# The last two blocks of a windowed-attention kernel: P turned on TensorE instead of by a DMA, and another order of the closing chains

## The chip, the cores and the metric

The kernel runs on one core of a Trainium2 chip. The metric is the device time of one execution in microseconds; lower is better. Before the change three runs gave 814.06, 810.92 and 812.58 us, a median of 812.58 us.

## The reference

```python
xn = layernorm(x)                                   # x: 1 x 2048 x 640
q  = (xn @ wq) -> 32 heads of 192                    # wq: 640 x 6144
k, v = last 512 rows of k_cache, v_cache             # per head 512 x 192
p  = softmax(q @ k.T * 192**-0.5)                    # per head 2048 x 512
s  = concat(p @ v) @ wo                              # wo: 6144 x 640
r  = xn @ w_r;  idx = the two rows with the largest r
y  = (silu(xn[idx] @ w_gate) * (xn[idx] @ w_up)) @ w_down * sigmoid(r[idx])
g  = silu(xn + y added into rows idx)
out = x + s * g
```

Nearly all of the work is attention: 32 heads, 2048 tokens, a window of 512 keys, and the projections into and out of the heads. The two-row expert part is small and lies long before the end.

## The kernel before

Heads are taken in pairs. A *step* is a group of four heads, a span of 512 tokens and a pair of heads; it is cut into two *blocks* of 256 tokens (two token tiles, a = 0 and 1, of 128 tokens). There are 64 steps and 128 blocks. A block b does, for each of its two token tiles, the scores (S, line 366, six matmuls into a PSUM tile of two banks), their row maximum on VectorE (M, line 371), and the exponentials on ScalarE (E, line 376, two instructions, one for each head). The exponentials are written as bf16 into `p_ring`, a ring of two blocks. The product with V needs P with the keys on the partitions, so P has to be turned. Line 380 does that for both token tiles with one DMA transpose on SP's queue (sixteen 128 x 128 tiles), issued behind the second E of the block, into `pT_ring`, a ring of three blocks.

Two blocks later P V is multiplied (called P or O in the order, line 393, 32 matmuls into two PSUM banks). A column of ones in V gives the softmax's sum beside the product. VectorE takes its reciprocal (line 400), and the product is scaled, for one head by VectorE (line 404) and for the other by ScalarE (line 407), into `o_ring`. The scaled O is turned as well, by a DMA transpose of six tiles (line 410), or, for the last two blocks, on TensorE (T, line 420, six transposes) with a copy out of PSUM by ScalarE (line 421). Six blocks later the output projection (W, line 434, 24 matmuls) reads turned O of two blocks: items 120 and 121 read blocks 120 and 122, items 122 and 123 read blocks 121 and 123, items 124 and 125 read blocks 124 and 126, items 126 and 127 read blocks 125 and 127. An item is half of the 640 output columns for two token tiles u = 0 and 1.

In the last head group each item is finished at once: VectorE multiplies it with g (line 460, one instruction for each u), and GpSimd adds `s_acc`, which by then holds x plus all earlier groups (line 465, a full row of 640 columns, after the odd item). The result goes out by DMA on GpSimd's queue, for the last four token tiles on SP's (line 466). Items 126 and 127 add their halves by themselves (line 462), on GpSimd for 126 and on VectorE for 127, and send them on SP's and ScalarE's queues (line 463).

PSUM is four pools: two tiles of two banks for scores ("s"), one tile of two banks for the q projection ("q"), two single banks for O and W ("o"). A W item or a turned tile of the end may be put into any of them; it then waits for the reader of the tile that stood there.

The order of the instructions on every engine is the order in which the program issues them; nothing rearranges it. Blocks 12 to 125 follow `BLOCK`; blocks 126 and 127 and the closing work follow the tokens of `LAST`, read by `last()`. In a token such as `W.122.q` or `O.126.va` the first number is the block or item, letters behind it name the bank or the engines (v VectorE, a ScalarE). SP's queue works in order: a DMA that waits for its data holds back those behind it.

Of the kernel before, what the change touches and what calls it, by code (L numbers as in the profile page):

```python
# [9 lines left out]
ALU = mybir.AluOpType  # L10
AX = mybir.AxisListType
ET = mybir.EngineType
FP32 = mybir.dt.float32
BF16 = mybir.dt.bfloat16
# [7 lines left out]
def kernel(ctx, tc, A_x, A_k_cache, A_v_cache, A_wq, A_wo, B_x, B_w_r, B_w_gate, B_w_up, B_w_down, out):  # L22
    nc = tc.nc
    P = 128
    _, S, D = A_x.shape
# [3 lines left out]
    W = min(4096, max(256, Sk // 4))  # L29
# [11 lines left out]
    KB = W // HK  # L41
# [9 lines left out]
    out_v = out.flatten_outer_dims().rearrange("(n p) d -> p n d", p=P)  # L51
# [5 lines left out]
    def pool(name, bufs, **kw):  # L57
        return ctx.enter_context(tc.tile_pool(name=name, bufs=bufs, **kw))
# [10 lines left out]
    ps_s = pool("ps_s", 2, space=bass.MemoryType.PSUM)  # L69
# [4 lines left out]
    def f_tile(shape, dtype, name, kind="q"):  # L74
        return banks[kind].tile(shape, dtype, name=name, tag="f")
# [3 lines left out]
    s_acc = big.tile([P, NTB, D], FP32, name="s_acc")  # L79

    RP, RO, RT, RV, VC = 3, 3, 7, 3, Dh + 4
    p_ring = big.tile([P, 2, 2, KB, 2, HK], BF16, name="pexp")
    pT_ring = big.tile([P, RP, 2, KB, P], BF16, name="pT")
# [20 lines left out]
    def half(r):  # L104
        return slice(r * HK, (r + 1) * HK)
# [56 lines left out]
    for _ in range(22):  # L162
# [5 lines left out]
        out=ident_f, in_=ident_f, compare_op=ALU.not_equal, fill=1.0, base=0,  # L168
        pattern=[[-1, P]], channel_multiplier=1,
    )  # L170
    ident = const.tile([P, P], BF16, name="ident")
# [115 lines left out]
    NS = len(steps)  # L287
    NB = 2 * NS
    HEAD = 12
    qT_of = {}  # L290
    fin_x = {}
    fin_pool = {}
# [76 lines left out]
    def row_max(b, a):  # L369
        nm_of[b, a] = small.tile([P, 2], FP32, name="nm")  # L370
        rm = nc.vector.tensor_reduce(out=nm_of[b, a], in_=s_of[b, a], axis=AX.X, op=ALU.max, negate=True)  # L371
        last_max["ins"], last_max["S"] = rm.ins, s_no[b, a]

    def exps(b, a):
        for hh in range(2):
            nc.scalar.activation(out=p_ring[:, b % 2, a, :, hh, :].rearrange("p (x j) e -> p x j e", x=2),  # L376
                                 in_=s_of[b, a][:, hh, :].rearrange("p (j e x) -> p x j e", j=NJ, x=2),
                                 func=ACT.Exp, bias=nm_of[b, a][:, hh:hh + 1], scale=1.0)
        if a == 1:
            nc.sync.dma_start_transpose(out=pT_ring[:, b % RP].rearrange("p a k t -> p (a k) t"),  # L380
                                        in_=p_ring[:, b % 2].rearrange("p a k h e -> p (a k h e)"))

    o_of = {}

    def o_products(b, between=None):
        g, t5, pr = steps[b // 2]
        o_of[b] = [f_tile([P, 2, W // 2], FP32, "o_ps", "o") for _ in range(2)]
        for a in range(2):
            if a == 1 and between is not None:
                between()  # L390
            for k in range(KB):
                for r in range(2):
                    nc.tensor.matmul(o_of[b][r][:, a, 0:Dh + 1], lhsT=pT_ring[half(r), b % RP, a, k, :],  # L393
                                     rhs=v_ring[half(r), (g * PAIRS + pr) % RV, k, 0:Dh + 1],
                                     start=(k == 0), stop=(k == KB - 1))

    def o_scaled(b, engines):
        rl = small.tile([P, 2, 2], FP32, name="rl")
        for r, e in sorted(enumerate(engines), key=lambda c: c[1]):
            nc.vector.reciprocal(out=rl[:, r], in_=o_of[b][r][:, :, Dh])  # L400
            o_sb = o_ring[:, b % RO, 3 * r:3 * r + 3].rearrange("p c a e -> p a c e")
            src = o_of[b][r][:, :, 0:Dh].rearrange("p a (c e) -> p a c e", e=HK)
            if e == "v":
                nc.vector.tensor_tensor(out=o_sb, in0=src, in1=rl[:, r].unsqueeze(2).unsqueeze(3).to_broadcast([P, 2, 3, HK]), op=ALU.mult)  # L404
            else:
                for a in range(2):
                    nc.scalar.activation(out=o_sb[:, a], in_=src[:, a], func=ACT.Copy, scale=rl[:, r, a:a + 1])  # L407
# [16 lines left out]
    def w_of(k):  # L424
        sp, up, h = k // 4, (k // 2) % 2, k % 2
        g, t5 = divmod(sp, NT5)
        return g, t5 * 4 + 2 * up, slice(h * HD, (h + 1) * HD), [4 * sp + 2 * pr + up for pr in range(PAIRS)]

    def w_products(k, w_ps):
        g, n, cs, bs = w_of(k)  # L430
        for pr in range(PAIRS):
            for c in range(CC):
                for r in range(2):
                    nc.tensor.matmul(w_ps[r][:, 0:HD], lhsT=oT_ring[half(r), bs[pr] % RT, c, :], rhs=grp[g][("wo", pr)][half(r), c, cs],  # L434
                                     start=(pr == 0 and c == 0), stop=(pr == PAIRS - 1 and c == CC - 1))

    def fin_tiles(n):
        if n not in fin_t:
            fin_t[n] = (fin_pool["t"].tile([P, 2, D], FP32, name="fin_t"), [fin_pool["o"].tile([P, D], BF16, name="fin_o") for _ in range(2)])
        return fin_t[n]  # L440

    def w_item(k, act=False, where="o", last=False):
        g, n, cs, _ = w_of(k)
        if where == "o":
            w_ps = [f_tile([P, W], FP32, "w", "o") for _ in range(2)]
        else:
            w_t = f_tile([P, 2, W], FP32, "w") if where == "q" else ps_s.tile([P, 2, W], FP32, name="w", tag="sc")
            w_ps = [w_t[:, u] for u in range(2)]
        w_products(k, w_ps)
        for u in range(2):  # L450
            src, acc = w_ps[u][:, 0:HD], s_acc[:, n + u, cs]
            if g == 0 and act:
                nc.scalar.copy(out=acc, in_=src)
            elif g == 0:
                nc.vector.tensor_copy(out=acc, in_=src)
            elif g < NG - 1:
                nc.vector.tensor_tensor(out=acc, in0=acc, in1=src, op=ALU.add)  # L457
            else:
                t, o = fin_tiles(n)
                nc.vector.tensor_tensor(out=t[:, u, cs], in0=src, in1=xn[:, n + u, cs], op=ALU.mult)  # L460
                if last:
                    (nc.vector if k % 2 else nc.gpsimd).tensor_tensor(out=o[u][:, cs], in0=t[:, u, cs], in1=s_acc[:, n + u, cs], op=ALU.add)
                    (nc.sync, nc.scalar)[u].dma_start(out=out_v[:, n + u, cs], in_=o[u][:, cs])
                elif k % 2 == 1:
                    nc.gpsimd.tensor_tensor(out=o[u], in0=t[:, u], in1=s_acc[:, n + u, :], op=ALU.add)  # L465
                    (nc.sync if n >= NTB - 4 else nc.gpsimd).dma_start(out=out_v[:, n + u, :], in_=o[u])
# [41 lines left out]
    copies = {"a": nc.scalar.copy, "v": nc.vector.tensor_copy}  # L508
# [102 lines left out]
    M = {}  # L611
# [210 lines left out]
    def m_gate(n):  # L822
        def a():
            M["tz"] = M["s"].tile([P, D], FP32, name="tz", tag="t2")
            nc.scalar.activation(out=M["tz"], in_=xn[:, n, :], func=ACT.Tanh)

        def b():
            nc.vector.scalar_tensor_tensor(out=xn[:, n, :], in0=M["tz"], scalar=1.0, in1=xn[:, n, :], op0=ALU.add, op1=ALU.mult)
        return a, b
# [29 lines left out]
    for n in range(NTB):  # L859
        bg[71 + 2 * n].append(m_add(n))  # L860
        a, b = m_gate(n)
# [33 lines left out]
    banks["o"] = pool("ps_o", 2, space=bass.MemoryType.PSUM)  # L895
    for b in range(HEAD, NB - 2):
        for token in BLOCK:
# [11 lines left out]
            elif token == "P":  # L909
                def between():  # L910
                    for f in bg.pop(b, []):
                        f()
# [5 lines left out]
    def last(token):  # L918
        op, *n = token.split(".")
        e = n[-1] if n and n[-1].isalpha() else None  # L920
        n = [int(c) for c in n if not c.isalpha()]
        if op == "S":
            scores(*n)
        elif op == "M":
            row_max(*n)
        elif op == "E":
            exps(*n)
        elif op == "P":
            o_item(n[0], e)
        elif op == "O":  # L930
            o_products(n[0])
            o_scaled(n[0], e)
        elif op == "T":
            o_turn(n[0], copies[e])
        elif op == "W":
            w_item(n[0], where=e or "o", last=n[0] >= NB - 2)
        else:
            flush(n[0])

    LAST = """  # L940
    S.126.0 M.126.0 W.120 E.126.0 S.126.1 M.126.1 P.124.va E.126.1 B.126
    S.127.0 M.127.0 W.121.q E.127.0 P.125.va S.127.1 M.127.1 E.127.1 B.127
    W.122.q O.126.va W.123.s T.126.a O.127.va W.124.s T.127.a W.125.s W.126.q W.127
    """.split()
    for token in LAST:
        last(token)
# [31 lines left out]
```

## Time and profile before

| | |
|---|---|
| three runs | 810.92 to 814.06 us, median 812.58 us |
| profiled execution, own time | 812.12 us |
| its span | 810.3 us |
| TensorE clock granted, mean | 0.997 |
| TensorE busy | 784.5 us, 97% of the span |
| VectorE busy | 585.8 us, 72% |
| ScalarE busy | 528.2 us, 65% |
| GpSimd busy | 311.5 us, 38% |
| DMA queue with the transposes | 93.0% of 16 engines' span |

The profiled execution takes 1.8 us longer than its span, from the first to the last instruction. Times in what follows are us from the start of the span. A line of the timeline merges instructions of one kind that follow each other: start, duration, engine, line of the kernel, operation, tile written <- tiles read, count, and in square brackets the idle time of the engine before them and what ended it. In the lines by group the numbers behind the bar are busy us and the mean ns of one instruction, then idle time of the engine before them. "Landing" is the time from a DMA's issue to its completion.

### The profile page before, as it was taken

What the parts mean: (1) busy time and instruction counts of PE and PEld (TensorE: products, weight loads), DVE (VectorE), ACT (ScalarE), POOL (GpSimd) and SP (SyncE); (2) the same over time, 40 slices, a digit from 0 to 9 for tenths busy, and PEclk for the clock granted to TensorE, in tenths of its full rate; (3) what the DMA queues carried; (4) which work ended last, traced back from release to release, by engine and by line L of the source; (5) the groups of instructions that cost most, each with busy time, mean ns of one, the idle gap of its engine ahead of it and who ended that gap; (6) DMA issues with size and microseconds to landing.
All of it is one profiled execution on the core that took longest, in us unless ns stands there. A gap on an engine that the chain in (4) does not pass through costs nothing.

```text
span 810.3 us, 26575 instructions
## 1 busy us (share of the span) xinstructions
PE 784.5 (97%) x11338; PEld 580.1 (72%) x11338; DVE 585.8 (72%) x1083; ACT 528.2 (65%) x963; POOL 311.5 (38%) x244
## 2 busy tenths in 40 slices
PE   8799899999999999999999999999999999999995
PEld 4366577777777777777777777777777777777773
DVE  7686588887777767767767677777777776776673
ACT  5677566666656766666666667767777776666661
POOL 1312120011110101001011799959995423555854
PEclk9999999999999999999999999999999999999998
DMA  7997998799999999999998999989999899998983
GB/s 192 190 173 165 196 172 165 143 183 170 182 188 181 172 214 199 193 178 206 196 205 154 175 182 181 161 157 181 154 193 176 150 185 176 198 187 160 191 155 76
DMA packets 446807, 142.81 MB, mean 176 GB/s; under 512 B 414180, under 2 KB 446184, under 8 KB 446688
## 3 DMA queue, kind: packets, MB, share of 16 engines
q1 hardware_dynamic: 436912, 131.71, 93.0%
q10 hardware_dynamic: 8816, 6.88, 3.2%
q0 software_dynamic: 960, 2.52, 1.1%
q8 instruction: 89, 1.46, 0.7%
q14 instruction: 30, 0.25, 0.1%
HBM read 39.98 MB, written 2.62 MB: 53 GB/s over the span
## 4 chain that ended last, share of the span: by engine, by line
PE 84%; DMA 7%; DVE 4%; ACT 3%; issue 2%; POOL 0%; SPq 0%; DVEq 0%; ACTq 0%; POOLq 0%
PE w L434 23%; PE q_ps L339 21%; PE o_ps L393 18%; PE s L366 18%; DMA pT<-pexp 6%; DVE nm L371 2%; PE q_ps L308 2%; ACT pexp L376 1%; PE warm_ps L163 1%; DMA xnT<-xn 1%; ACT o_sb L407 1%; DMA wo_g<-in_A_wo_dram 1%; ACT qT L351 0%; ACT qT L314 0%; PE gu_ps L754 0%
## 5 line engine op out<-in xcount | busy, mean ns | idle before, releaser
L371 DVE TENSOR_REDUCE nm<-s 128x2 f32<-128x1024 f32 x256 | 313.0, 1223 | 138.0 <-PE s L366 130.9
L376 ACT ACTIVATE pexp<-s,nm 128x512 bf16<-128x512 f32 x512 | 323.6, 688 | 97.7 <-DVE nm L371 54.2
L339 PE MATMUL q_ps<-xnT,wq_g 64*128 64x512 bf16 (+1 forms) x2340 | 232.6, 323 | 3.7 <-ACT qT L351 1.5
L434 PE MATMUL w<-wo_g,oT 64*128 64x320 bf16 x3072 | 232.4, 297 | 2.4 <-ACT o_sb L407 2.1
L366 PE MATMUL s<-kT,qT 64*128 64x512 bf16 x1536 | 211.8, 376 | 5.1 <-ACT pexp L376 3.9
L434 PEld LDWEIGHTS <-oT 64*128 64x128 bf16 x3072 | 173.2, 94 | 60.5 <-issue 5.0
L393 PEld LDWEIGHTS <-pT 64*128 64x128 bf16 x4096 | 179.2, 94 | 33.7 <-DMA pT<-pexp 6.2
L393 PE MATMUL o_ps<-v_sb,pT 64*128 64x193 bf16 x4096 | 197.9, 243 | 4.6 <-DMA pT<-pexp 4.4
L407 ACT ACTIVATE o_sb<-o_ps,rl 128x192 bf16<-128x192 f32 x256 | 93.6, 417 | 142.5 <-DVE rl L400 139.7
L339 PEld LDWEIGHTS <-wq_g 64*128 64x128 bf16 x2340 | 127.8, 99 | 48.8 <-issue 3.2
L151 POOL COPY wo_g<-wo_g 64x1920 bf16<-64x1920 bf16 x32 | 59.4, 1861 | 221.8 <-DMA wo_g<-in_A_wo_dram 201.1
L366 PEld LDWEIGHTS <-qT 64*128 64x128 bf16 x1536 | 85.7, 94 | 59.4 <-issue 6.0
L457 DVE TENSOR_TENSOR s_acc<-s_acc,w 128x320 f32<-128x320 f32 x192 | 85.0, 484 | 34.2 <-PE w L434 34.2
L351 ACT ACTIVATE qT<-q_ps 128x1024 bf16<-128x1024 f32 x114 | 92.4, 810 | 6.6 <-PE q_ps L339 1.9
L121 POOL COPY k_perm<-k_raw 128x768 bf16<-128x768 bf16 x30 | 25.0, 851 | 143.3 <-DMA k_raw<-in_A_k_cache_dram 110.8
L404 DVE TENSOR_TENSOR o_sb<-o_ps,rl 128x384 bf16<-128x384 f32 x128 | 71.4, 557 | 4.6 <-DVE rl L400 0.2
L818 POOL TENSOR_SCALAR yh<-y_bc,oh 128x640 bf16<-128x640 bf16 x32 | 60.8, 1901 | 3.3 <-DMA y_bc<-y_d 1.7
L819 POOL TENSOR_TENSOR xn<-xn,yh 128x640 bf16<-128x640 bf16 x32 | 45.4, 1418 | 2.7
L400 DVE RECIPROCAL rl<-o_ps 128x2 f32<-128x2 f32 x256 | 30.0, 158 | 20.7 <-PE o_ps L393 14.5
L881 POOL TENSOR_TENSOR s_acc<-s_acc,x_fin 128x640 f32<-128x640 f32 x16 | 22.4, 1397 | 31.9 <-DMA x_fin<-in_A_x_dram 31.4
L465 POOL TENSOR_TENSOR fin_o<-fin_t,s_acc 128x640 bf16<-128x640 f32 x14 | 21.5, 1537 | 24.3 <-DVE fin_t L460 17.8
L815 POOL TENSOR_SCALAR xn<-xn 128x640 bf16<-128x640 bf16 x16 | 29.4, 1838 | 0.8
(134 smaller groups left out, 252.0 us busy)
## 6 DMA issues: line engine op xcount, KB each, us to landing
wo_g<-in_A_wo_dram SPq DMA_DIRECT2D x32, 240.0 KB, 4.2
k_raw<-in_A_k_cache_dram SPq DMA_DIRECT2D x32, 192.0 KB, 3.4
v_sb<-in_A_v_cache_dram SPq DMA_DIRECT2D x32, 192.0 KB, 4.1
wq_g<-in_A_wq_dram SPq DMA_DIRECT2D x14, 288.0 KB, 3.9
wq_g<-in_A_wq_dram SPq DMA_DIRECT2D x14, 192.0 KB, 3.7
x_fin<-in_A_x_dram SPq DMA_DIRECT2D x16, 160.0 KB, 3.6
pT<-pexp SPq DMA_TRANSPOSE x128, 4.9
oT<-o_sb SPq DMA_TRANSPOSE x126, 3.5
```

The lines of the kernel that those rows point to most:

```text
L151: nc.gpsimd.tensor_copy(out=grp[g][("wo", pr)][half(1), cs, :], in_=grp[g][("wo", pr)][half(0), cs, :])
L339: mm = nc.tensor.matmul(q_ps[k][:, 0:n] if type(q_ps) is list else q_ps[:, k, 0:n], lhsT=wq[half(r), dc, c:2 * Dh:3], rhs=xnT[half(r), tok ...
L351: nc.scalar.activation(out=out, in_=q_ps[:, :, 0:n], func=ACT.Copy, scale=scale)
L366: nc.tensor.matmul(s_of[b, a][:, r, :], lhsT=qT_of[i][half(r), c, u * P:(u + 1) * P], rhs=grp[g][("kT", pr)][half(r), :, c, :], start=(c = ...
L371: rm = nc.vector.tensor_reduce(out=nm_of[b, a], in_=s_of[b, a], axis=AX.X, op=ALU.max, negate=True)
L376: nc.scalar.activation(out=p_ring[:, b % 2, a, :, hh, :].rearrange("p (x j) e -> p x j e", x=2), in_=s_of[b, a][:, hh, :].rearrange("p (j ...
L393: nc.tensor.matmul(o_of[b][r][:, a, 0:Dh + 1], lhsT=pT_ring[half(r), b % RP, a, k, :], rhs=v_ring[half(r), (g * PAIRS + pr) % RV, k, 0:Dh ...
L404: nc.vector.tensor_tensor(out=o_sb, in0=src, in1=rl[:, r].unsqueeze(2).unsqueeze(3).to_broadcast([P, 2, 3, HK]), op=ALU.mult)
L407: nc.scalar.activation(out=o_sb[:, a], in_=src[:, a], func=ACT.Copy, scale=rl[:, r, a:a + 1])
L434: nc.tensor.matmul(w_ps[r][:, 0:HD], lhsT=oT_ring[half(r), bs[pr] % RT, c, :], rhs=grp[g][("wo", pr)][half(r), c, cs], start=(pr == 0 and ...
L457: nc.vector.tensor_tensor(out=acc, in0=acc, in1=src, op=ALU.add)
L818: nc.gpsimd.tensor_scalar(out=yh, in0=M["y_bc"][:, j, :], scalar1=M["oh"][:, n, j:j + 1], scalar2=None, op0=ALU.mult)
```

## The change

P of blocks 124, 125 and 126 (`SPLIT`) is still turned by DMA, but in two DMA transposes of eight tiles, each issued behind its own E, instead of one of sixteen behind the second. P of block 127 is no longer turned by DMA: for each token tile eight TensorE transposes write a PSUM tile of the "s" pool (`U`, new function `p_turn`), and ScalarE copies it to `pT_ring`.

The order of `LAST` changes. Item 120 goes into the "q" bank. E of block 126, tile 1, stands ahead of O of block 124; S and M of block 127, tile 1, stand ahead of O of block 125 and E behind it. Item 122 precedes the first turn of P. The copy of turned O of block 126 goes from ScalarE to VectorE. Item 126 goes into "s" and item 127 into "q".

The closing additions change for items 124 to 127. Items 124 and 125 now each add their own halves on GpSimd and send them by SP, in four transfers of 320 columns instead of two of 640. Items 126 and 127 both add on VectorE; u = 0 goes out by SP, u = 1 by ScalarE's queue. (In `o_products` the letter "o" for the bank is what it was before.)

```diff
+    SPLIT = (NB - 4, NB - 3, NB - 2)
...
-        if a == 1:
+        if b in SPLIT:
+            nc.sync.dma_start_transpose(out=pT_ring[:, b % RP, a], in_=p_ring[:, b % 2, a].rearrange("p k h e -> p (k h e)"))
+        elif a == 1 and b < NB - 1:
             nc.sync.dma_start_transpose(out=pT_ring[:, b % RP].rearrange("p a k t -> p (a k) t"),
                                         in_=p_ring[:, b % 2].rearrange("p a k h e -> p (a k h e)"))
 
+    def p_turn(b, a, where, copy):
+        tp = f_tile([P, KB, P], BF16, "tp_p") if where == "q" else ps_s.tile([P, KB, P], BF16, name="tp_p", tag="sc")
+        for k in range(KB):
+            nc.tensor.transpose(out=tp[:, k, :], in_=p_ring[:, b % 2, a, k].rearrange("p h e -> p (h e)"), identity=ident)
+        copy(out=pT_ring[:, b % RP, a], in_=tp)
...
-                if last:
-                    (nc.vector if k % 2 else nc.gpsimd).tensor_tensor(out=o[u][:, cs], in0=t[:, u, cs], in1=s_acc[:, n + u, cs], op=ALU.add)
-                    (nc.sync, nc.scalar)[u].dma_start(out=out_v[:, n + u, cs], in_=o[u][:, cs])
+                if k >= NB - 4:
+                    (nc.vector if last else nc.gpsimd).tensor_tensor(out=o[u][:, cs], in0=t[:, u, cs], in1=s_acc[:, n + u, cs], op=ALU.add)
+                    (nc.scalar if last and u else nc.sync).dma_start(out=out_v[:, n + u, cs], in_=o[u][:, cs])
...
     LAST = """
-    S.126.0 M.126.0 W.120 E.126.0 S.126.1 M.126.1 P.124.va E.126.1 B.126
-    S.127.0 M.127.0 W.121.q E.127.0 P.125.va S.127.1 M.127.1 E.127.1 B.127
-    W.122.q O.126.va W.123.s T.126.a O.127.va W.124.s T.127.a W.125.s W.126.q W.127
+    S.126.0 M.126.0 W.120.q E.126.0 S.126.1 M.126.1 E.126.1 P.124.va B.126
+    S.127.0 M.127.0 W.121.q E.127.0 S.127.1 M.127.1 P.125.va E.127.1 W.122.q U.127.0.sa
+    O.126.vao U.127.1.sa W.123.s T.126.v O.127.vao W.124.s T.127.a W.125.s W.126.s W.127.q B.127
     """.split()
```

More of the change, by code (lines that the diff above doesn't have):

```diff
@@ L378, in exps, with o_products @@
                                  func=ACT.Exp, bias=nm_of[b, a][:, hh:hh + 1], scale=1.0)
-        if a == 1:
+        if b in SPLIT:
+            nc.sync.dma_start_transpose(out=pT_ring[:, b % RP, a], in_=p_ring[:, b % 2, a].rearrange("p k h e -> p (k h e)"))
+        elif a == 1 and b < NB - 1:
             nc.sync.dma_start_transpose(out=pT_ring[:, b % RP].rearrange("p a k t -> p (a k) t"),
                                         in_=p_ring[:, b % 2].rearrange("p a k h e -> p (a k h e)"))
+    def p_turn(b, a, where, copy):
[3 more added lines that the diff above has]
+        copy(out=pT_ring[:, b % RP, a], in_=tp)
     o_of = {}
-    def o_products(b, between=None):
+    def o_products(b, between=None, where="o"):
         g, t5, pr = steps[b // 2]
-        o_of[b] = [f_tile([P, 2, W // 2], FP32, "o_ps", "o") for _ in range(2)]
+        if where == "o":
+            o_of[b] = [f_tile([P, 2, W // 2], FP32, "o_ps", "o") for _ in range(2)]
+        else:
+            o_t = f_tile([P, 2, 2, W // 2], FP32, "o_ps") if where == "q" else ps_s.tile([P, 2, 2, W // 2], FP32, name="o_ps", tag="sc")
+            o_of[b] = [o_t[:, r] for r in range(2)]
         for a in range(2):
@@ L930, in last @@
         elif op == "O":
-            o_products(n[0])
-            o_scaled(n[0], e)
+            o_products(n[0], where=e[2])
+            o_scaled(n[0], e[0:2])
+        elif op == "U":
+            p_turn(n[0], n[1], e[0], copies[e[1]])
         elif op == "T":
```

## The prediction

> **What bounds the kernel now.** I read the slices of the span first, then the chain that ended last, then TensorE's timeline of the end, and last the DMA landings and the groups of the last 35 us.
>
> ```profile
> PE   8799899999999999999999999999999999999995
> PEclk9999999999999999999999999999999999999998
> ```
>
> TensorE is busy throughout and bounds the span, except in the last slice (20 us), where it is half idle and its clock dips. The change touches nothing ahead of block 124, so only this end counts. The chain there:
>
> ```profile
> 772.38 11.79 DMA pT<-pexp x2
> ...
> 789.06 5.39 DMA pT<-pexp
> ```
>
> Here the chain runs through the DMA transposes of P (blocks 124, 125, then 127), not through TensorE. TensorE's own timeline, with the blocks that I put to the lines by counting back from the end:
>
> ```profile
> 775.26 0.83 PE L366 MATMUL s<-kT,qT 64*128 64x512 bf16 x6
> 776.46 1.81 PE L434 MATMUL w<-wo_g,oT 64*128 64x320 bf16 x24 [0.38 <-ACT o_sb L407]
> ...
> 779.30 1.50 PE L393 MATMUL o_ps<-v_sb,pT 64*128 64x193 bf16 x31 [0.16 <-DVE fin_t L460]
> ...
> 784.22 1.52 PE L393 MATMUL o_ps<-v_sb,pT 64*128 64x193 bf16 x32 [1.14 <-DMA pT<-pexp]
> 785.58 0.81 PE L366 MATMUL s<-kT,qT 64*128 64x512 bf16 x6
> 786.22 1.79 PE L434 MATMUL w<-wo_g,oT 64*128 64x320 bf16 x24
> 788.01 1.52 PE L393 MATMUL o_ps<-v_sb,pT 64*128 64x193 bf16 x32
> 789.38 1.79 PE L434 MATMUL w<-wo_g,oT 64*128 64x320 bf16 x24
> 791.10 0.51 PE L420 MATMUL tp_o<-ident,o_sb 128*128 128x128 bf16 x6
> 794.50 1.99 PE L393 MATMUL o_ps<-v_sb,pT 64*128 64x193 bf16 x32 [2.89 <-DMA pT<-pexp]
> 796.28 3.03 PE L434 MATMUL w<-wo_g,oT 64*128 64x320 bf16 x24
> 799.24 0.51 PE L420 MATMUL tp_o<-ident,o_sb 128*128 128x128 bf16 x6
> 799.68 5.06 PE L434 MATMUL w<-wo_g,oT 64*128 64x320 bf16 x72
> ```
>
> From S of block 126 (775.26) to the last matmul (799.68 + 5.06 = 804.74) are 29.48 us. Idle with a named cause: 0.38 + 0.16 + 1.14 + 2.89 = 4.57 us. The pitch of the work, start to start: S 0.64 (785.58 to 786.22), O 1.37 (788.01 to 789.38), W 1.69 (5.06 / 3), T 0.44 (799.24 to 799.68). Behind the long wait the same work is slower: O of block 127 takes 1.78 and W 124 2.96, together 1.68 us too long. Why, the windows show (columns: stretch, its length, busy TensorE, weight loads, VectorE, ScalarE, GpSimd, granted clock, DMA):
>
> ```profile
> 783.00:784.00 1.00, 0.08 (x2) 0.00 (x0) 0.88 (x2) 0.00 (x0) 0.30 (x1) 1.00 1.15 170
> ...
> 796.00:797.00 1.00, 1.00 (x12) 0.70 (x10) 0.44 (x3) 0.22 (x1) 0.56 (x1) 0.50 0.00 0
> ...
> 799.00:800.00 1.00, 1.00 (x18) 0.58 (x14) 0.57 (x2) 0.21 (x1) 0.00 (x0) 1.00 0.00 0
> ```
>
> The granted clock is 0.50 after the 2.89 us wait and 1.00 again by 799; the 1.14 us wait left it at 1.00. [...]
>
> **The change, part by part.**
>
> *TensorE's work.* Four S, eight W, four O and two T stay: 4 x 0.64 + 8 x 1.69 + 4 x 1.37 + 2 x 0.44 = 22.44 us. Added are sixteen transposes (U). Six take 0.44 us, so sixteen take 1.17 us, all of it in TensorE's row, covered by nothing. Without any wait TensorE would end at 775.26 + 22.44 + 1.17 = 798.87, which is 5.87 us sooner. The clock's 1.68 us goes with the wait that brought it.
>
> *Do waits come back?* I laid the new order out with the pitches above: O 125 at 782.6, W 122 at 783.9, U of tile 0 at 785.6, O 126 at 786.2, U of tile 1 at 787.6, W 123 at 788.2, T 126 at 789.9, O 127 at 790.3, W 124 at 791.7, T 127 at 793.4, W 125, 126, 127 at 793.8, 795.5, 797.2. Each needs something by then, priced from these rows:
>
> ```profile
> L376 ACT ACTIVATE pexp<-s,nm 128x512 bf16<-128x512 f32 x10 | 6.3, 686 | 3.1 <-DMA pT<-pexp 2.0 <-DVE nm L371 1.1
> L371 DVE TENSOR_REDUCE nm<-s 128x2 f32<-128x1024 f32 x5 | 6.1, 1216 | 0.4 <-PE s L366 0.4
> L460 DVE TENSOR_TENSOR fin_t<-w,xn 128x320 f32<-128x320 f32 x16 | 7.2, 486 | 7.2 <-PE w L434 7.2
> L407 ACT ACTIVATE o_sb<-o_ps,rl 128x192 bf16<-128x192 f32 x10 | 3.7, 417 | 8.3 <-DVE rl L400 8.3
> L421 ACT COPY oT<-tp_o 128x768 bf16<-128x768 bf16 x2 | 1.6, 798 | 3.4 <-PE tp_o L420 3.4
> ...
> L283 ACT COPY xnT<-tp 128x640 bf16<-128x640 bf16 x6 | 4.1, 698 | 3.4 <-PE tp L282 3.4
> ...
> L277 DVE COPY kT<-tp_k 128x768 bf16<-128x768 bf16 x1 | 0.6, 556 | 0.4 <-PE tp_k L276 0.4
> ...
> 776.30 1.26 ACT L376 ACTIVATE pexp<-s,nm 128x512 bf16<-128x512 f32 x2
> 778.29 1.26 ACT L376 ACTIVATE pexp<-s,nm 128x512 bf16<-128x512 f32 x2 [0.73 <-DMA pT<-pexp]
> ...
> 777.82 3.12 SPq L380 DMA_TRANSPOSE pT<-pexp  x1
> ...
> 789.06 3.25 SPq L380 DMA_TRANSPOSE pT<-pexp  x1
> ...
> DMA to landing us min/median/max: 4.3/5.4/6.7
> ...
> DMA to landing us min/median/max: 2.7/2.9/3.6
> ```
>
> The last two rows are P's transposes (sixteen tiles) and O's (six tiles) near the end. Eight tiles lie between: I take 3.4 us (2.9 plus two tenths of the difference), with bounds 2.9 and 6.7. On SP one sixteen-tile issue holds the queue 3.1 to 3.25 us; halves should hold it half as long each, so the two together cost SP nothing new. The ring of P is written two blocks later, and its E waited 0.73 us for the transpose of block 124 (778.29); with halves that wait goes.
>
> - Second half of block 125: E ends at 777.56, issued 777.7, lands 781.1; O 125 reads it from 783.3. Spare 2.2 us; at 5.4 us spare 0.2; at 6.7 a stall of 1.1.
> - Tile 1 of block 126: E 126.1 now stands ahead of O 124's scaling on ScalarE and ends near 781.1, its half lands 784.5; O 126 reads it from 786.9. O turned of blocks 124 and 125 moves behind both halves on SP's queue, issued near 782.7 and 785; W 124 and W 126 read them nine and ten us later.
> - E 127.1 is queued on ScalarE behind E 127.0 (to 783.1) and the scaling of O 125 (784.2 to 785.0) and ends at 786.3; U of tile 1 comes at 787.6. Spare 1.3.
> - The copies of turned P on ScalarE: 1024 columns, by the step from 640 to 768 (698 to 798 ns) 1.0 us each. The first ends at 787.4; W 123 waits for its bank at 788.2: spare 0.8. Behind it on ScalarE stand the scaling of O 126 (to 788.6) and the second copy (to 789.6); O 127 reads that from 791.0: spare 1.4.
> - T 126's copy on VectorE, 0.56 us, stands behind W 123's multiplications (0.97, to 790.8), ends 791.4; W 124 reads it from 792.5: spare 1.1.
> - T 127 at 793.4 needs O 127 scaled, near 792.7: spare 0.7, the smallest. Its copy ends 794.7, W 126 reads it from 796.3.
> - The bank changes (120 and 127 to "q", 126 to "s") free item 120 of the 0.38 us wait and otherwise wait for multiplications that end over 1 us sooner.
>
> So I allow 0.2 us for hand-overs, between 0 and 2.5 (a late half and two of the small spares missed by 0.7).
>
> *The tail.* It was one item's VectorE work:
>
> ```profile
> L462 POOL TENSOR_TENSOR fin_o<-fin_t,s_acc 128x320 bf16<-128x320 f32 x2 | 1.9, 974 | 0.0
> ...
> 804.78 0.49 DVE L460 TENSOR_TENSOR fin_t<-w,xn 128x320 f32<-128x320 f32 x1 [0.66 <-PE w L434]
> 805.31 1.00 DVE L462 TENSOR_TENSOR fin_o<-fin_t,s_acc 128x320 bf16<-128x320 f32 x1
> ...
> 806.75 0.63 DVE L462 TENSOR_TENSOR fin_o<-fin_t,s_acc 128x320 bf16<-128x320 f32 x1
> ...
> span 810.3 us, 26575 instructions
> ```
>
> From the last matmul to the last addition's end (807.38) 2.64 us, from there to the span's end 2.92 us, which stays (one ScalarE DMA at the end, as before). Now VectorE also has item 126's two additions. GpSimd does four half additions of items 124 and 125 at 0.97 us, and they run up to about 800, beside item 126's. VectorE's first addition took 1.00 us beside a GpSimd addition, the second 0.63. So item 126 takes 2 x 0.49 + 2 x 1.00 = 2.98 us, starting 1.65 us ahead of TensorE's end, then item 127 2 x 0.49 + 2 x 0.63 = 2.24: the last addition ends 2.98 + 2.24 - 1.65 = 3.57 us behind TensorE, 0.93 more than before. All at 0.63 it would be 0.2 more, all at 1.00 1.7 more. The smaller output transfers ride on SP, which is free then; they end sooner than the last addition.
>
> [...]
>
> *Sum.* -5.87 + 0.2 + 0.93 = -4.74 us. The profiled execution took 812.12 us (0.46 under the median of the runs, well within their spread): 807.4 us, 0.6% faster.
>
> **The rivals.**
>
> 1. *The wait moves into the closing ladder.* Late halves (6.7 us to landing: 1.1 us), hand-overs missing the 0.7 and 0.8 us spares by as much again (1.4 us): TensorE gains 3.4 instead of 5.7, and the time is 809.7. For it: ScalarE and VectorE alternate strictly and each copy lies on the way; the landing row's maximum is on record. Against: every spare is reckoned from measured durations of the same instructions, and only 0.7 and 0.8 us are small.
> 2. *The tail takes it.* VectorE's eight closing instructions become the bound, every addition waiting for a GpSimd one (0.97 us each for four instead of two at 0.37): about 3.1 us more, 810.5. The 0.63 us row speaks against it for item 127, whose additions come when GpSimd is done.
> [...]
> 4. *The halves come no sooner.* The DMA engines are full until block 125 (1.15 in the window at 783), so a half issued early might land with the whole. Then the 1.14 us wait stays and E 126 keeps its 0.73 us, but block 127's wait and the clock are gone: 807.4 + 1.5 = 808.9.
>
> **How the numbers follow.** What a measurement here can tell from no change is about 0.5%, 4.06 us: faster is below 808.5. The forecast (807.4, with 805.5 to 808.5 around it) gets 0.60; rivals 1, 2 and 4, or parts of them together, 0.30, most of which lies between 808.5 and 810.5, a little below; rival 3 and any other that ends slower 0.07; a better end, with no losses and additions at 0.63 (806.4 or, with the runs' spread of 1.6 below the median, 805), 0.03. Faster 0.62, same 0.30, slower 0.08. The range is 805.0 to 811.0: the no-loss case with the runs' spread below, rival 2 with half a microsecond of it above.
>
> **What would show it.** In the changed trace O 125 follows S 127.1 and O 127 follows T 126 without idle time ended by a DMA of P; the granted clock is 1.00 to the last matmul; TensorE ends near 799 on this clock; ScalarE's copies of P take 1.0 us; the eight-tile transposes land in about 3.4 us; from the last matmul to the span's end it is about 6.5 us instead of 5.56. The forecast is wrong if T 127, W 123 or O 127 wait for ScalarE by a microsecond, if additions of items 126 and 127 all take 1 us, or if the clock drops.

## The result, and the profile after

The changed kernel takes 808.38 us (median of five runs, 807.77 to 809.43) against 812.72 us before: a ratio of 0.9947, 95% interval 0.9929 to 0.9965. The profiled execution took 807.77 us, its span is 806.0 us, against 810.3. The slices of the span in the page of the kernel after:

```profile
span 806.0 us, 26621 instructions
...
PE   8799899999999999999999999999999999999997
...
PEclk9999999999999999999999999999999999999999
```

The dip in the last slice is smaller, and the clock stays at 1.00 to the last matmul. TensorE's timeline at the end, in the kernel after:

```profile
776.77 0.82 PE L367 MATMUL s<-kT,qT 64*128 64x512 bf16 x6
...
784.04 1.53 PE L406 MATMUL o_ps<-v_sb,pT 64*128 64x193 bf16 x32
785.39 1.81 PE L447 MATMUL w<-wo_g,oT 64*128 64x320 bf16 x24
787.14 0.62 PE L389 MATMUL tp_p<-ident,pexp 128*128 128x128 bf16 x8
787.69 1.52 PE L406 MATMUL o_ps<-v_sb,pT 64*128 64x193 bf16 x32
789.14 0.62 PE L389 MATMUL tp_p<-ident,pexp 128*128 128x128 bf16 x8
789.70 1.80 PE L447 MATMUL w<-wo_g,oT 64*128 64x320 bf16 x24
791.43 0.51 PE L433 MATMUL tp_o<-ident,o_sb 128*128 128x128 bf16 x6
791.88 1.52 PE L406 MATMUL o_ps<-v_sb,pT 64*128 64x193 bf16 x32
...
795.40 5.06 PE L447 MATMUL w<-wo_g,oT 64*128 64x320 bf16 x72
```

No line carries an idle time in brackets any more: TensorE goes from block 126's first scores (776.77) to the last matmul (795.40 + 5.06 = 800.46) without a stall. I call this stretch the *TensorE part*: 23.69 us, against 29.48 before. The rest, from the last matmul to the end of the span, I call the *tail*: 806.0 - 800.46 = 5.54 us, against 5.56. So the end as a whole is 5.8 us shorter, and the span only 4.3, because block 126 begins 1.51 us later than in the profile of before, at the end of some 770 us in which both kernels issue the same instructions. That start moves by up to 5.5 us from one execution to the next (775.26 to 780.74 us), as much as the change's own effect, so I judge the experiments with one run by the TensorE part and the tail. These repeat: four profiles of kernels that give TensorE the same work in the same order (after twice, and the two experiments on the tail below) have TensorE parts of 23.69 to 23.70 us.

### The profile page after: what moved, and what is told of

It reads as the page before. It is cut to its first block, busy times and chain, and to the rows that moved or that the text cites. A ratio compares the mean times of both kernels' runs of the same rounds, so it can differ in the third digit from the quotient of the medians.

```text
span 806.0 us, 26621 instructions
## 1 busy us (share of the span) xinstructions
PE 783.0 (97%) x11354; PEld 579.1 (72%) x11354; DVE 591.0 (73%) x1086; ACT 529.3 (66%) x964; POOL 310.1 (38%) x244
## 4 chain that ended last, share of the span: by engine, by line
PE 85%; DVE 5%; DMA 4%; ACT 3%; issue 2%; POOL 0%; SPq 0%; ACTq 0%; DVEq 0%; POOLq 0%
PE w L447 24%; PE q_ps L340 21%; PE o_ps L406 18%; PE s L367 18%; DVE nm L372 2%; DMA pT<-pexp 2%; PE q_ps L309 2%; ACT o_sb L420 1%; ACT pexp L377 1%; PE warm_ps L163 1%; DMA xnT<-xn 1%; DMA oT<-o_sb 1%; DMA wo_g<-in_A_wo_dram 1%; DMA v_sb<-in_A_v_cache_dram 0%; ACT qT L315 0%
## 5 line engine op out<-in xcount | busy, mean ns | idle before, releaser
L478 POOL TENSOR_TENSOR fin_o<-fin_t,s_acc 128x640 bf16<-128x640 f32 x12 | 18.5, 1540 | 17.7 <-DVE fin_t L473 11.1
```

## The experiments

**How much of the 29.48 us was the clock?** The kernel before, unchanged:

> The kernel before, unchanged, once more. The TensorE part is the time from the first score matmul of block 126 to the last matmul; it was 29.48 us before and is 23.69 after. Theory (the clock drop follows the 2.89 us wait, but by the phase of a window): the wait of about 2.9 us ahead of O of block 127 is there again; the drop to 0.50 may be there (TensorE part 29.5) or not (27.8). Rival (the drop belongs to this kernel's work, whatever the phase): 29.5, the clock again 0.50 for about 3 us.

TensorE's timeline in that execution:

```profile
780.53 0.82 PE L366 MATMUL s<-kT,qT 64*128 64x512 bf16 x6
...
799.44 1.52 PE L393 MATMUL o_ps<-v_sb,pT 64*128 64x193 bf16 x32 [2.53 <-DMA pT<-pexp]
800.80 1.79 PE L434 MATMUL w<-wo_g,oT 64*128 64x320 bf16 x24
...
802.97 5.06 PE L434 MATMUL w<-wo_g,oT 64*128 64x320 bf16 x72
```

The wait is there (2.53 us), the drop is not: O 127 has its usual 1.36 us pitch and W 124 1.73. TensorE part 27.50 us. So the clock's loss is not tied to this work alone. It is frequent all the same: of the eleven executions of the kernel before that were timed beside the last experiments, ten have a mean granted clock of 0.996 or 0.997, as the first profile has, and one 0.999, at 810.33 us the fastest of them. No profile here without the drop has a mean under 0.998 (in before and after it falls behind the last matmul too, at 809.04 and 805.58 us, and the mean counts that), so the drop comes in most executions, not in all, and is worth some 1.7 us.

The wait filled with matmuls that nothing reads:

```diff
-    W.122.q O.126.va W.123.s T.126.a O.127.va W.124.s ...
+    W.122.q O.126.va W.123.s T.126.a F O.127.va W.124.s ...
+        elif op == "F":
+            fill_t = ps_s.tile([P, 2, W], FP32, name="fill", tag="sc")
+            for _ in range(12):
+                nc.tensor.matmul(fill_t[:, 0, :], lhsT=ident, rhs=xnT[:, 0:4, 0, :], start=True, stop=True)
```

> Twelve matmuls of 512 columns that nothing reads are put into the 2.89 us wait of the kernel before; no other work changes. Theory (two terms: the wait, and the clock that the idle time brings): the clock stays 1.00, O of block 127 still starts when its transpose lands, then O and W 124 take 1.4 and 1.7 us instead of 1.78 and 2.96; TensorE part 27.8 us. Rival (O and W 124 were slow for another reason): they stay slow, 29.5 us.

TensorE's timeline with the wait filled:

```profile
776.54 0.83 PE L366 MATMUL s<-kT,qT 64*128 64x512 bf16 x6
...
792.83 2.75 PE L936 MATMUL fill<-xnT,ident 128*128 128x512 bf16 x12
795.52 1.52 PE L393 MATMUL o_ps<-v_sb,pT 64*128 64x193 bf16 x32
...
799.05 5.06 PE L434 MATMUL w<-wo_g,oT 64*128 64x320 bf16 x72
```

TensorE part 27.57 us, at full clock, as the theory has it. Since the unfilled wait also kept its clock once, one execution doesn't show that the filling did it.

The traces' records of the granted clock show what goes with the drop. In the profile of before full clock is granted first at 6.91 us; the clock falls to 0.50 at 795.39, is 1.00 again at 798.80, and falls to 0.50 at 809.04, behind the last matmul. The changes lie 788.48, 3.41 and 10.24 us apart, which are 231, 1 and 3 steps of 3.413 us. In that of after full clock comes at 6.86 and the fall behind the last matmul at 805.58: 798.72 us, 234 such steps. What the expectation calls a window is this step, as far as these two traces show it. The two experiments below that drop ahead of the last matmul, the one without TensorE turns and the one with turned O of block 125 issued behind the last half, are at 0.50 for 3.4 us as well (795.9 to 799.3 and 797.1 to 800.5, by windows of 1 us). The lines, with the columns of the prediction's windows, show the step that holds most of the wait and the one behind it in the kernel before; then the step with the wait of 2.24 us, with turned O of block 125 behind the last half; then that in the second execution of before; last the step in the kernel after in which TensorE ends.

```profile
791.97:795.39 3.42, 0.89 (x22) 0.90 (x24) 0.13 (x1) 0.47 (x1) 3.10 (x3) 1.00 0.65 163
795.39:798.80 3.41, 3.41 (x36) 2.27 (x32) 0.79 (x3) 0.73 (x2) 0.90 (x2) 0.50 0.13 48
...
793.70:797.11 3.41, 1.31 (x26) 1.16 (x28) 0.41 (x4) 0.17 (x1) 2.88 (x3) 1.00 0.62 124
...
797.70:801.11 3.41, 1.67 (x38) 1.60 (x40) 0.10 (x2) 0.04 (x1) 3.02 (x3) 1.00 0.58 149
...
798.76:802.17 3.41, 1.71 (x26) 0.98 (x22) 3.12 (x6) 0.00 (x0) 1.51 (x2) 1.00 0.40 119
```

TensorE idled 2.5 us of the first of these steps, 2.1, 1.7 and 1.7 of the last three. The steps with 2.5 and 2.1 us were followed by a clock of 0.50, those with 1.7 by 1.00. The steps of the three waits begin 0.36 (of 2.89), 0.14 (of 2.24) and 0.79 us (of 2.53) behind the wait's start. So in these profiles the gap's length alone does not decide (2.24 us was followed by the drop, 2.53 was not), but how much of it falls into one step.

**Which part of the change carries the gain?** First only the turn of block 127's P on TensorE, with the new closing line:

```diff
-    SPLIT = (NB - 4, NB - 3, NB - 2)
+    SPLIT = ()
-    S.126.0 M.126.0 W.120.q E.126.0 S.126.1 M.126.1 E.126.1 P.124.va B.126
-    S.127.0 M.127.0 W.121.q E.127.0 S.127.1 M.127.1 P.125.va E.127.1 W.122.q U.127.0.sa
+    S.126.0 M.126.0 W.120 E.126.0 S.126.1 M.126.1 P.124.va E.126.1 B.126
+    S.127.0 M.127.0 W.121.q E.127.0 P.125.va S.127.1 M.127.1 E.127.1 W.122.q U.127.0.sa
```

> P of block 127 turned on TensorE, the closing line and the additions as after, but whole DMA transposes for blocks 124 to 126 and the first two lines of the order (the scores and O of blocks 126, 127) as before. Theory (the turn of P of block 127 carries the gain): the wait of 2.89 us and the clock's 1.68 us go, 1.17 us of transposes come, the wait of about 1.1 us ahead of O 125 stays; TensorE part 26.1 us. Rival (the order and the halves carry it): the wait only moves to the turned copies, 28 us or more.

Then the new order too, but whole transposes for blocks 124 to 126 (only the first two lines of that diff):

> After, but blocks 124 to 126 turned by one DMA transpose each as before. Theory (the halves keep O 125 and E 126 from waiting): O 125, which now comes 1.6 us sooner than the transpose landed before, waits about 1.6 us, and the last exponentials come later by as much; TensorE part 25.3 to 25.8 us. Rival (the halves cost as much to land as wholes, 4.8 against 4.9 us, and buy nothing): 23.7 us, no wait.

TensorE's timeline with the old front:

```profile
778.65 0.82 PE L367 MATMUL s<-kT,qT 64*128 64x512 bf16 x6
...
787.60 1.52 PE L406 MATMUL o_ps<-v_sb,pT 64*128 64x193 bf16 x32 [1.12 <-DMA pT<-pexp]
...
799.59 5.06 PE L447 MATMUL w<-wo_g,oT 64*128 64x320 bf16 x72
```

and with whole transposes:

```profile
777.34 0.82 PE L367 MATMUL s<-kT,qT 64*128 64x512 bf16 x6
...
786.34 1.52 PE L406 MATMUL o_ps<-v_sb,pT 64*128 64x193 bf16 x32 [1.54 <-DMA pT<-pexp]
...
797.69 5.06 PE L447 MATMUL w<-wo_g,oT 64*128 64x320 bf16 x72
```

TensorE parts 26.00 and 25.41 us; the first is 0.1 us from its theory, the second within it. With the clock at 1.00 up to the last matmul in all four, and the parts added in this order, the steps are 27.50 (the second execution of before) to 26.00 with the turn and the new closing line, 25.41 with the order of the first two lines, 23.69 with the halves: 1.50, 0.59 and 1.72 us. The added transposes of 1.1 us are already in the first step.

The whole transposes make O 125 wait 1.54 us; in halves it doesn't wait. The transfer that decides is the one behind block 125's last exponentials, a half in the kernel after (issued at 779.26) and a whole in the kernel with whole transposes (779.89), in both about 0.2 us behind these exponentials. From issue to landing the half and the whole take:

```profile
DMA to landing us min/median/max: 5.2/5.2/5.2
...
DMA to landing us min/median/max: 6.4/6.4/6.4
```

So this half is issued no sooner than the whole, but lands 1.24 us sooner (5.16 against 6.40). By the times of O 125's matmuls it does so in every profile: at most 5.5 us in the nine with halves there, 6.3 to 6.5 in the five with a whole. The rest comes from the first half, which has long landed: sixteen of O 125's matmuls need only that one, and they take 0.68 us.

**Is the turn on TensorE needed, once the order is new?** P of block 127 by two half DMAs:

```diff
-    SPLIT = (NB - 4, NB - 3, NB - 2)
+    SPLIT = (NB - 4, NB - 3, NB - 2, NB - 1)
-    ... E.127.1 W.122.q U.127.0.sa O.126.vao U.127.1.sa W.123.s ...
+    ... E.127.1 W.122.q O.126.vao W.123.s ...
```

> After, but P of block 127 is turned by two half DMA transposes like blocks 124 to 126; no TensorE transposes of P. TensorE part (first score matmul of block 126 to the last matmul) is 23.69 us after. Theory (with the new order the turn on TensorE is no longer needed, since the last exponentials end 4 us ahead of O of block 127): 1.17 us of transposes go, the last half lands 3.6 to 4.8 us after its exponentials and O of block 127 waits 0 to 1.0 us for it; TensorE part 22.5 to 23.5 us. Rival (turning on TensorE is what closes the wait, as the change has it): the wait is 2 us or more, 24.5 us or more.

TensorE's timeline of this kernel:

```profile
777.76 0.83 PE L367 MATMUL s<-kT,qT 64*128 64x512 bf16 x6
...
795.07 0.85 PE L406 MATMUL o_ps<-v_sb,pT 64*128 64x193 bf16 x16 [2.66 <-DMA pT<-pexp]
795.75 3.30 PE L447 MATMUL w<-wo_g,oT 64*128 64x320 bf16 x24
...
799.54 5.06 PE L447 MATMUL w<-wo_g,oT 64*128 64x320 bf16 x72
```

SP's timeline of it:

```profile
788.72 1.34 SPq L423 DMA_TRANSPOSE oT<-o_sb  x1
790.16 2.57 SPq L381 DMA_TRANSPOSE pT<-pexp  x1
```

and the landing of that last half, from the view of its line:

```profile
DMA to landing us min/median/max: 4.9/4.9/4.9
```

My theory fell: a wait of 2.66 us, on tile 1's half alone (sixteen matmuls), the clock at 0.50 behind it from 795.9 to 799.3 (W 124 takes 3.30 instead of 1.80), TensorE part 26.84 us. The last exponentials end at 788.72, the half stands behind turned O of block 125 on SP's queue until 790.16, and lands 4.9 us later. To tell the queue's share, turned O of block 125 was issued behind the half:

```diff
-    ... P.125.va E.127.1 W.122.q ...
+    ... O.125.vao E.127.1 R.125 W.122.q ...      # R: o_turned(125)
```

> The kernel without TensorE turns (P of block 127 in two halves by DMA), with turned O of block 125 issued behind the last half instead of ahead of it. Theory (of the 2.66 us wait there, 1.45 us was the place behind turned O on SP's queue, the rest the 4.9 us to landing): the wait is 1.2 us, the clock stays 1.00, TensorE part 23.7 us, as after. Rival (the queue's place costs nothing, the landing is late anyway): 2.7 us again, 25 us or more.

TensorE's timeline of this one:

```profile
778.92 0.82 PE L367 MATMUL s<-kT,qT 64*128 64x512 bf16 x6
...
795.80 0.85 PE L406 MATMUL o_ps<-v_sb,pT 64*128 64x193 bf16 x16 [2.24 <-DMA pT<-pexp]
...
799.97 5.32 PE L447 MATMUL w<-wo_g,oT 64*128 64x320 bf16 x72
```

and the landings of its last two halves, tile 0's the shortest, tile 1's the longest:

```profile
DMA to landing us min/median/max: 3.7/4.8/5.9
```

The queue's place is worth 0.4 us, not 1.45: issued as soon as its data are there, the half lands 5.9 us later instead of 4.9. The wait remains (2.24), the clock falls to 0.50 again, TensorE part 26.37 us. So in neither place on the queue is a DMA early enough for tile 1; an order that brings its exponentials sooner was not tried. Why the half takes a microsecond longer when turned O follows it is open. For tile 0 the DMA is early enough:

```diff
-        if b in SPLIT:
+        if b in SPLIT or (b, a) == (NB - 1, 0):
-    ... E.127.1 W.122.q U.127.0.sa O.126.vao U.127.1.sa ...
+    ... E.127.1 W.122.q O.126.vao U.127.1.sa ...
```

> After, but only token tile 1 of block 127 is turned on TensorE; tile 0 goes by a half DMA transpose. Theory: tile 0's exponentials end 7 us ahead of O of block 127, so its half is hidden even at 5.2 us to landing; 0.55 us of transposes and 1.0 us of ScalarE go; TensorE part 23.1 us, no wait. Rival (the half stands behind others on SP's queue and comes late): a wait ahead of O of block 127, 23.7 us or more.

TensorE's timeline with one tile turned:

```profile
776.00 0.82 PE L367 MATMUL s<-kT,qT 64*128 64x512 bf16 x6
...
793.97 5.06 PE L447 MATMUL w<-wo_g,oT 64*128 64x320 bf16 x72
```

TensorE part 23.03 us, no wait, as expected. (The tail of this kernel is longer; see the timed versions.)

**The tail.** The additions and output transfers as before, the rest as after:

```diff
-                if k >= NB - 4:
-                    (nc.vector if last else nc.gpsimd).tensor_tensor(...)
-                    (nc.scalar if last and u else nc.sync).dma_start(...)
+                if last:
+                    (nc.vector if k % 2 else nc.gpsimd).tensor_tensor(...)
+                    (nc.sync, nc.scalar)[u].dma_start(...)
```

> After, with the additions and output transfers of items 124 to 127 as before (full rows on GpSimd for 124 and 125, GpSimd for 126, VectorE for 127). The tail is the time from the last matmul to the span's end: 5.56 us before, 5.54 after. Theory by what the trace after shows (additions alone take 0.49 us, beside GpSimd 1.0 to 1.2): the two orders are equal, 5.3 to 5.7 us. Rival (the prediction's term: item 126 on VectorE costs 0.93 us): 4.6 us.

The span was 809.9 us, the last matmul ended at 804.44, the tail is 5.46 us: equal within 0.1 us. Then the kernel after with GpSimd relieved of two transfers:

```diff
-                    (nc.sync if n >= NTB - 4 else nc.gpsimd).dma_start(out=out_v[:, n + u, :], in_=o[u])
+                    (nc.sync if n >= NTB - 6 else nc.gpsimd).dma_start(out=out_v[:, n + u, :], in_=o[u])
```

> After, with the output transfers of items 122 and 123 issued by SP instead of GpSimd, which takes 2 x 0.86 us off GpSimd's row ahead of the additions of items 124 and 125. Theory (VectorE's first addition took 1.16 us because it overlapped GpSimd's last ones, which ended at 800.3): GpSimd ends before VectorE's first addition or in its first tenths, that addition takes 0.49 to 0.7 us and the tail 4.9 to 5.1 us. Rival (the first addition is slow for another reason): 1.16 us again, tail 5.5 us.

VectorE's timeline in the kernel after:

```profile
799.47 1.16 DVE L475 TENSOR_TENSOR fin_o<-fin_t,s_acc 128x320 bf16<-128x320 f32 x1
...
801.06 0.49 DVE L475 TENSOR_TENSOR fin_o<-fin_t,s_acc 128x320 bf16<-128x320 f32 x1
...
802.92 0.49 DVE L475 TENSOR_TENSOR fin_o<-fin_t,s_acc 128x320 bf16<-128x320 f32 x1
```

GpSimd's:

```profile
796.95 3.32 POOL L475 TENSOR_TENSOR fin_o<-fin_t,s_acc 128x320 bf16<-128x320 f32 x4
```

VectorE's with GpSimd relieved:

```profile
799.28 0.49 DVE L475 TENSOR_TENSOR fin_o<-fin_t,s_acc 128x320 bf16<-128x320 f32 x1
...
802.06 0.49 DVE L475 TENSOR_TENSOR fin_o<-fin_t,s_acc 128x320 bf16<-128x320 f32 x1
```

and GpSimd's:

```profile
797.62 1.69 POOL L475 TENSOR_TENSOR fin_o<-fin_t,s_acc 128x320 bf16<-128x320 f32 x2 [0.42 <-DVE fin_t L473]
```

GpSimd's last addition ended at 800.27 in the one and at 799.31 in the other, and VectorE's first addition took 1.16 and 0.49 us: the overlap is the cause. (In the kernel without TensorE turns the first addition started 0.03 us before GpSimd's last one ended, and took 0.49 us as well.) The last addition ends 2.95 and 2.28 us behind the last matmul, 0.67 sooner. The tail falls only to 5.23 us, short of the theory's 4.9 to 5.1, since from the last addition to the span's end it was 2.59 us in the profile of after and 2.95 here. That last stretch lay between 2.58 and 3.02 us in all fourteen profiles. It repeats within 0.02 us in the three kernels that were profiled twice (before 2.92 and 2.94, after 2.59 and 2.58, one tile turned 3.02 and 3.00), so it belongs to the kernel; what sets it is open.

**Timed versions.** In one job, beside eleven runs of before (median 812.85 us): the kernel after again, the one with one tile turned, and that with the transfers on SP as well.

> The kernel after, unchanged, timed in five rounds beside the same runs of before. Theory (the end is 3.8 us shorter than before where the clock held, 5.8 where it dropped): a ratio of 0.993 to 0.9955; TensorE part 23.7 us. Rival (the first interval was luck of the loop ahead of the end, which moves by 1 to 5 us between executions): 0.997 or more.

> After with only token tile 1 of block 127 turned on TensorE, timed. Theory: 0.6 us less TensorE work than after, on the path: a ratio to before of 0.992 to 0.995, some 0.7 us below after. Rival (the tail takes it): the same time as after.

> The kernel with only tile 1 turned on TensorE, and with the output transfers of items 122 and 123 on SP's queue as well. Theory: both savings add, 0.66 us of TensorE's part and 0.67 us of VectorE's first addition: TensorE part 23.0 us, last addition 2.3 us behind the last matmul, a ratio to before of 0.991 to 0.994. Rival (the end of the span is set by the output transfers, not by the last addition): no gain over the kernel with one tile turned.

| kernel | median, range | ratio to before | 95% interval |
|---|---|---|---|
| after | 808.38, 806.33 to 810.68 | 0.9937 | 0.9919 to 0.9955 |
| one tile turned | 807.24, 805.89 to 811.0 | 0.9941 | 0.9918 to 0.9964 |
| one tile turned, transfers on SP | 806.55, 805.53 to 806.71 | 0.9919 | 0.9905 to 0.9934 |

The gain of the change is confirmed; the profile of after in this job has a TensorE part of 23.70 us and a tail of 5.52. Turning one tile cannot be told from after in time; its interval covers the forecast saving and none. Its two profiles show that the rival is right in part: the TensorE part is 23.03 and 23.09 us, 0.6 less than after, but the tail is 5.97 and 5.95 us, 0.43 more, all of it in the last stretch. With the transfers as well the median is the lowest of all, 1.8 us under after, but the intervals of the two overlap, so that a gain over after is not shown by the times. Its profile has both savings, on TensorE:

```profile
776.50 0.82 PE L367 MATMUL s<-kT,qT 64*128 64x512 bf16 x6
...
794.54 5.06 PE L447 MATMUL w<-wo_g,oT 64*128 64x320 bf16 x72
```

and on VectorE:

```profile
801.39 0.49 DVE L475 TENSOR_TENSOR fin_o<-fin_t,s_acc 128x320 bf16<-128x320 f32 x1
```

TensorE part 23.10 us, the last addition 2.28 us behind the last matmul, tail 5.20 us.

## Why the prediction was right

The forecast was 807.4 us, 0.6% faster; measured were 808.38 us and 0.53% (0.63% in the second job). The mechanism was right: the wait for block 127's P goes, no new wait comes, and the clock's loss goes with it. Between the two profiles the sum came out as -5.79 us in the TensorE part (forecast -5.67), -0.02 in the tail (forecast +0.93) and +1.51 from the later start of block 126 (not in the sum): -4.30 us of span, forecast -4.74.

- *TensorE's work and its waits:* laid out at 23.61 us plus 0.2 for hand-overs, measured 23.69. No hand-over of the ladder cost anything; the spares reckoned as the smallest, 0.7 and 0.8 us, held. Rivals 1, 2 and 4 did not come: O 125, W 123 and O 127 start without idle time, and the tail did not grow. ScalarE's copies of P took 1.01 us each, as reckoned:

```profile
L390 ACT COPY pT<-tp_p 128x1024 bf16<-128x1024 bf16 x2 | 2.0, 1012 | 0.1
```

- *The halves' landing:* mis-sized. I took 3.4 us, between six tiles and sixteen; in the trace after the six halves landed so:

```profile
DMA to landing us min/median/max: 3.1/4.8/5.2
```

  It cost nothing, but by little. The half that matters, tile 1 of block 125, was issued at 779.26 and landed at 784.42, and O 125, started at 784.04, needs it 0.68 us later: of the spare of 2.2 us 0.3 was left. In two profiles of the kernels with one tile turned nothing was left, and O 125's second sixteen matmuls came 0.07 us late. What the halves bring is a landing 1.24 us sooner than that of a whole and products of tile 0 that need not wait for tile 1; without them O 125 waited 1.54 us. So rival 4 was right to doubt the 3.4 us, though the half did come sooner than the whole.
- *The clock:* the term of 1.68 us is real in most executions of before and absent in some. The wait of 2.89 us ahead of it was on record; what in a wait brings the drop no run had shown then. The profiles show it behind steps with 2.5 and 2.1 us of idle time, and full clock behind steps with 1.7. U and T ran at 1.00 in the kernel after, so the slower end, which was given 0.07, did not come. Whether the clock takes TensorE's transposes like other matmuls is not shown by that, since U and T take at most 1.1 us of any 3.41, less than the 1.7 us of plain idling that did no harm.
- *The tail:* mis-sized. I added 0.93 us and measured none, for two reasons. The last addition ended 2.95 us behind the last matmul instead of 3.57 (before: 2.64), and the stretch behind it, which I took to stay at 2.92 us, was 2.59. The additions without GpSimd beside them take 0.49 us; the 0.63 that I read as one without GpSimd had overlapped GpSimd's last addition by some 0.3 us, and of item 126's two additions only the first was slowed (1.16). Eight instructions took 4.46 us instead of 5.22. In the kernel after VectorE's slowed addition started less than 0.1 us behind GpSimd's last one and ended 0.36 behind its end. The two additions of before that overlapped GpSimd's (1.00 and 0.63 us) ended 0.36 and 0.35 us behind the end of GpSimd's as well: whether they overlapped GpSimd's by 0.3, 0.65 or 0.8 us, all three ended as far behind it.
- *What the sum left out:* the start of block 126, 1.51 us later in this execution. The forecast compared one execution with one, and such a difference is larger than its terms for the hand-overs and the tail together. The too large tail and this drift are of opposite sign, so that the total came out as near as it did by luck.

## What to carry to other kernels

A DMA transpose that stands on the path can be split, so that the first part is done early and only the last part is waited for. Here the last half, issued when the whole would be, landed 1.2 us sooner, and the products that need only the first half went ahead. Turn on TensorE the piece for which no DMA is early enough, and look at what the last additions of two engines overlap (here 1.16 us for one that did, 0.49 without). Where a loop ahead of the change wanders by microseconds, compare the changed stretch itself, from a first to a last instruction, and leave the whole time to many runs; then look at the stretch behind it too, which here took back two thirds of a saving.

## What was not expected

Half transposes of 8 tiles landed in 4.8 us (median) where whole ones of 16 near there took 5.4 and those of 6 tiles 2.9: the price is not proportional to the tiles. Gaps of 2.24, 2.66 and 2.89 us on TensorE were followed by a granted clock of 0.50 for 3.4 us, one of 2.53 us was not; the profiles with 2.24, 2.53 and 2.89 us differ in how much idle time falls into one step of 3.41 us: 2.1, 1.7 and 2.5 us. Block 126 began between 775.26 and 780.74 us in executions with the same instructions ahead of it; why is open.
